# Fourier filter and two MLPs on one core: conversions leave the last column steps, and the way back follows the filter more closely

## The chip, the core and the metric

The kernel runs on one core of one Trainium2 chip. The time is that of one execution on the device, in microseconds; three runs of each kernel stand side by side, and the profile is that of one further execution. Engines are named as in the profile: PE is TensorE (PEld its weight loads), DVE is VectorE, ACT is ScalarE, POOL is GpSimd, SP the queue that issues most transfers.

## The reference, cut to what matters

```python
def _attn_ref(x, filt_r, filt_i):            # x: 4 x 3136 x 256
    X = np.fft.rfft(x, axis=1)
    F = (filt_r + 1j * filt_i)[None, :, :]
    return np.fft.irfft(X * F, n=x.shape[1], axis=1)

def _moe_ref(x, U, V, w_ch1, w_ch2):         # U: 3136 x 32, V: 32 x 3136, w: 256 x 1024 x 256
    h = x.transpose(0, 2, 1) @ U @ V
    u = x + h.transpose(0, 2, 1)
    return u + np.maximum(u @ w_ch1, 0.0) @ w_ch2

def _moe2_ref(x, g_ln, w_ch1, w_ch2):
    xn = (x - mean) / sqrt(var + 1e-6) * g_ln
    return x + np.maximum(xn @ w_ch1, 0.0) @ w_ch2
```

The three are applied one after the other. The weights and U, V come as 64-bit floats, seen by the kernel as pairs of 32-bit words.

## The kernel before

The transform of length 3136 is done as two stages of matmuls with tables, 28 groups of 112 positions. Batch 0 has a path of its own, the class `First`, in plain f32; batches 1 to 3 (`fft`) run later beside the MLPs. For batch 0 `rows` does the first stage and leaves its result in `big`, and `columns` does the second stage, the filter and the first half of the way back, two groups at a time: 14 pairs of groups.

A step j of `columns` has four parts. TensorE turns a pair back (line 502, `psz`), ScalarE copies it (`z0`). The pair turned in step j-1 goes through the table `e` (line 513, `ps2`), and `filt` copies its halves exchanged and negated on ScalarE (`xs` or `hh`) and multiplies `ps2` by the real filter on VectorE (line 225, into `ya` or `hl`; the tiles alternate). `total` multiplies the exchanged halves by the imaginary filter (line 492) and adds them (line 493), for the pair that was filtered one step earlier (`ADDL`). The way back multiplies a summed pair with the table in `d` (line 522, `ps3`, two halves of channels), copies the result into `big` on ScalarE, and adds up 64 columns on VectorE (line 528 the first time, then 530); `BACKL` says how late it is. Line 522 has the summed pair as its stationary operand, so a sum must be complete before it. In the first four steps `u_half` makes the spectrum of U (`pst`, line 462) for `uf`, from which ScalarE copies columns into `d`.

PSUM has eight banks: three in `ps_h`, four in `ps_o`, one in `ps_t`. Each engine runs its instructions in the order of the program; a matmul whose bank is still being read waits, and all behind it.

Weights are converted from 64-bit to 32-bit by a generator, `stagger`, which is called once for each *slot*. A job starts every four slots (`PACE`). In its first slot ScalarE reads the two words (lines 768 and 769), in the next four VectorE has one operation each (755, 757, 759, 761), with the last of them GpSimd multiplies (773), one slot later it adds (775); four slots on ScalarE copies the high part (`w1h`, `w2h`, `vh`), and in the next the low part is made on GpSimd (846, 885). So every fourth slot is a job change: a copy and two conversions on ScalarE, line 761, and three GpSimd operations that follow. `ROWSLOTS` and `COLSLOTS` say how many slots stand behind each step of `rows` and `columns`; the other slots stand in the long loop, one behind m1 and one at the end of each step.

The long loop runs 25 blocks of tokens through both MLPs, eight steps each: `m1` (six matmuls, `psh`, then `hh` on ScalarE and `hl` on VectorE), and `m2` of two steps before (`pso`). Between them stand the inverse transform of units of tokens (`psu`) and, early, the parts of batch 0 that are still to be turned (`psw`, `wt`, lines 572 and 574). Each w1b half is centred by two matmuls (line 855, `psw` from `wg`), which stand where the job's slot stands.

Of the kernel before, what the change touches and what calls it, by code (L numbers as in the profile page):

```python
# [10 lines left out]
F32 = mybir.dt.float32  # L11
# [9 lines left out]
P = 128  # L21
# [9 lines left out]

WARM, KEEP = 9, 2
ULAG, UTURN = 1, (0, 1, 2, 3)
ADDL, BACKL = 2, 4
AHEAD = 3
FETCHES = (0, 1, 3, 6)

SLOTS, UAHEAD = 8, 2
PACE = 4
ROWSLOTS = (0, 1, 1, 1, 1, 2, 2, 3, 3, 4, 4, 5)  # L40
COLSLOTS = (0, 0) + tuple(range(18))
VSTEP = 9
DIRECT = 4

# [94 lines left out]
def fft_mixer_kernel(ctx: ExitStack, tc: tile.TileContext, x, U, V, flt, w1, w2, gln, w1b, w2b,  # L139
# [7 lines left out]
    ps_h = ctx.enter_context(tc.tile_pool(name="ps_h", bufs=3, space=PSUM))  # L147
    ps_o = ctx.enter_context(tc.tile_pool(name="ps_o", bufs=4, space=PSUM))
    ps_t = ctx.enter_context(tc.tile_pool(name="ps_t", bufs=1, space=PSUM))
# [15 lines left out]
    def acopy(o, i, scale=1.0):  # L165
        nc.scalar.activation(out=o, in_=i, func=AF.Copy, scale=scale)  # L166
# [198 lines left out]
    class First:  # L365
# [76 lines left out]
        def u_half(self, h):  # L442

            if h:
                self.zs, uf = (mp.tile([P, 4 * D], F32, tag="x2t", name=nm, bufs=2)[:, :NM * R] for nm in ("zs", "uf"))
                self.uf = uf.rearrange("p (g r) -> p g r", r=R)
            n = 14 * R
            ps = ps_t.tile([P, 512], F32, tag="t", name="pst")
            for k in range(14):
                g = 14 * h + k  # L450
                nc.tensor.transpose(ps[:PP, k * R:(k + 1) * R], self.zu[:, g * PP:(g + 1) * PP], ident[:R, :R])
            zs = self.zs[:PP, h * n:(h + 1) * n]
            acopy(zs, ps[:PP, :n])
            yield
            ps = ps_t.tile([P, 512], F32, tag="t", name="pst")
            a = 0 if h else R
            if a:
                nc.tensor.matmul(ps[:, :a], self.e[:, 1], zs[:, :a], start=True, stop=True)
            nc.tensor.matmul(ps[:, a:n], self.e[:, 0], zs[:, a:], start=True, stop=True)
            for lo, hi, wc in ((14, 28, w_sb[:, 0:1]),) if h else ((0, 1, w_sb[:, 1:2]), (1, 14, w_sb[:, 0:1])):  # L460
                src = ps[:, (lo - 14 * h) * R:(hi - 14 * h) * R].rearrange("p (g r) -> p g r", r=R)
                nc.vector.tensor_scalar(out=self.uf[:, lo:hi], in0=src, scalar1=wc, scalar2=None, op0=ALU.mult)
# [14 lines left out]
        def columns(self):  # L477
# [17 lines left out]
            for j in range(n + BACKL):  # L495
                if j < n:
                    i = n - 1 - j
                    ps = ps_o.tile([P, 512], F32, tag="o", name="psz")
                    for g in range(2):
                        for dh in range(KT):  # L500
                            a = g * D + dh * P
                            nc.tensor.transpose(ps[:PP, a:a + P], self.big[:, dh, (2 * i + g) * PP:(2 * i + g + 1) * PP], ident)
                    zt[i] = wide(F32, "fin", "z0", D, 3)
                    acopy(flat(zt[i]), ps[:PP])
                if 0 < j <= n:
                    i = n - j
                    z = zt.pop(i)
                    ps = ps_h.tile([P, 512], F32, tag="h", name="ps2")
                    if i == 0:
                        for g in range(2):  # L510
                            nc.tensor.matmul(ps[:, g * D:(g + 1) * D], self.e[:, 1 - g], z[:, g], start=True, stop=True)
                    else:
                        nc.tensor.matmul(ps, self.e[:, 0], flat(z), start=True, stop=True)
                    sp.filt(i, ps, True)
                total(j)
                if j >= BACKL:
                    i = n + BACKL - 1 - j
                    ya = sp.y.pop(i)[0]
                    for dh in range(KT):
                        ps = (ps_h if dh else ps_o).tile([P, 512], F32, tag="h" if dh else "o", name="ps3")  # L520
                        for g in range(2):
                            nc.tensor.matmul(ps[:, g * w:(g + 1) * w], dealt(ya[:, g], dh), slot(2 * i + g),
                                             start=True, stop=True)
                        pv = ps[:, :2 * w].rearrange("p (g w) -> p g w", w=w)
                        acopy(self.big[:, dh, 2 * i * PP:2 * (i + 1) * PP].rearrange("p (g w) -> p g w", w=PP), pv[:, :, :PP])
                        acc = self.t[:, dh]
                        if j == BACKL:
                            nc.vector.tensor_copy(acc, pv[:, :, PP:])
                        else:
                            nc.vector.tensor_tensor(out=acc, in0=pv[:, :, PP:], in1=acc, op=ALU.add)  # L530
                if j in UTURN:
                    next(turns[UTURN.index(j) // 2], None)
                self.filters(j + AHEAD)
                if BACKL - UAHEAD <= j < n + BACKL - UAHEAD:
                    i = n + BACKL - UAHEAD - 1 - j
                    for g in () if i else range(2):
                        acopy(slot(g)[:, PP:w], self.uf[:, g])
                    if i:
                        g = 2 * i % SLOTS
                        acopy(d0[:, g:g + 2, PP:w], self.uf[:, 2 * i:2 * i + 2])  # L540
                yield j
# [352 lines left out]
    with tc.manual_schedule():  # L894
# [24 lines left out]
        for j in first.columns():  # L919
            for _ in range(COLSLOTS.count(j)):  # L920
                next(pr)
# [55 lines left out]
        for idx in range(len(steps) + 2):  # L977
            if idx < len(steps):
                ph, f = steps[idx]
                if ph[0] == "a" and f == 0:  # L980
                    units_to(need(ph[1]))
                m1(ph, f)
                load_to(emitted)
                next(pr, None)
                if idx > FFT0:
                    credit += RATE if 1 not in tstk else 0.4
                    if credit >= 1:
                        credit -= 1
                        next(rest, None)
            for act in todo.pop(0) if todo else ():  # L990
                act()
            if idx >= 2:
                m2(*steps[idx - 2])
                if steps[idx - 2][1] == FT - 1:
                    end(steps[idx - 2][0])
            if idx < len(steps):
                if f in (3, 6) and ph in ahead:
                    units_to(need(ahead[ph]), 1)
                if idx in PARTS:
                    next(later, None)  # L1000
                if idx == UPARTS:
                    first.u_parts()
                next(pr, None)
# [32 lines left out]
```

## Time and profile before

| | |
|---|---|
| median of three runs | 1381.7 us (1380.94 to 1382.22) |
| the profiled execution | 1380.91 us, span 1379.1 us |
| stage `rows` | until 34.3 us |
| stage `columns` | 34.3 to 91 us, 18 steps |
| first units and long loop | from 92.64 us |
| granted TensorE clock | 1.00 in nearly all of the span |

The span is what the trace covers; the rest of the time lies around it. Times in the text below are those of this execution, from the start of its span. In rows of the order of time a bracket at the end says how long the engine had stood idle before and whom it waited for.

### The profile page before, as it was taken

The numbers are of one execution on the slowest core, as the hardware profiler recorded it, in microseconds if no ns is written. First come the engines' busy times: TensorE is split into PE (matmuls) and PEld (weight loads), VectorE is DVE, ScalarE is ACT, GpSimd is POOL, SyncE is SP. The second block draws the span as 40 slices with busy tenths as digits, with TensorE's granted clock in tenths as the row PEclk, the third lists the DMA queues.
The fourth block names the chain that finished last, engine by engine and source line by source line (L and its number), as shares of the span: only waits on it lengthen the run. The fifth ranks groups of instructions, "written<-read, shape, count | busy, mean of one in ns | idle before, by whom it ended". The sixth has DMA issues, their size and how long they took to land.

```text
span 1379.1 us, 18643 instructions
## 1 busy us (share of the span) xinstructions
PE 1345.5 (98%) x6870; PEld 1122.9 (81%) x6870; DVE 822.9 (60%) x1642; ACT 555.9 (40%) x1048; POOL 151.1 (11%) x145
## 2 busy tenths in 40 slices
PE   8879999999999999999999999999999999999998
PEld 7568778877888887888888888888888888888887
DVE  4778975577555547666555557665455455544554
ACT  4865444466433334554333335554222222222221
POOL 2236611022000001111000001110000000000000
PEclk9999999999999999999999999999999999999999
DMA  9735356565535534543345355453112112200111
GB/s 268 264 97 139 88 132 190 156 178 165 141 93 146 135 81 129 153 134 100 80 127 142 91 137 147 126 153 81 25 52 65 35 37 79 66 18 29 46 47 39
DMA packets 141595, 152.20 MB, mean 110 GB/s; under 512 B 61472, under 2 KB 117696, under 8 KB 141408
## 3 DMA queue, kind: packets, MB, share of 16 engines
q1 hardware_dynamic: 134880, 139.72, 35.9%
q0 software_dynamic: 5760, 10.10, 3.3%
q8 instruction: 54, 0.88, 0.3%
q10 hardware_dynamic: 864, 1.20, 0.2%
q14 instruction: 37, 0.30, 0.1%
HBM read 103.44 MB, written 47.54 MB: 109 GB/s over the span
## 4 chain that ended last, share of the span: by engine, by line
PE 85%; DVE 7%; ACT 3%; DMA 3%; issue 2%; SPq 0%; POOL 0%; ACTq 0%; DVEq 0%; POOLq 0%
PE psh L632 36%; PE pso L659 12%; PE pso L660 6%; PE pso L651 6%; PE pso L652 6%; PE pso L653 6%; PE psu L603 3%; PE ps L198 2%; PE ps L199 2%; PE ps L200 2%; ACT xs L166 1%; DMA f<-flt 1%; DVE x2t L693 1%; PE psu L605 1%; DVE hl L636 1%
## 5 line engine op out<-in xcount | busy, mean ns | idle before, releaser
L636 DVE SCALAR_TENSOR_TENSOR hl<-psh,hh 128x512 fp32r<-128x512 f32 (+1 forms) x400 | 270.9, 678 | 408.8 <-ACT hh L635 408.3
L635 ACT ACTIVATE hh<-psh 128x512 fp32r<-128x512 f32 (+1 forms) x400 | 235.1, 588 | 624.6 <-PE psh L632 619.0
L659 PE MATMUL pso<-wb,hh 128*128 128x512 f32 x784 | 285.3, 397 | 0.8 <-DVE x L673 0.7
L632 PE MATMUL psh<-ah,wb 128*128 128x512 f32 (+1 forms) x800 | 277.0, 388 | 0.0
L660 PE MATMUL pso<-wb,hl 128*128 128x256 f32 x784 | 220.2, 281 | 0.6 <-DVE hl L636 0.6
L632 PEld LDWEIGHTS psh<-ah,wb 128*128 128x128 f32 x800 | 149.8, 188 | 33.1
L659 PEld LDWEIGHTS pso<-wb,hh 128*128 128x128 f32 x784 | 147.4, 188 | 35.0 <-DVE x L673 3.1
L651 PE MATMUL pso<-hh,w2h 128*128 128x512 f32 (+1 forms) x400 | 156.3, 391 | 1.0 <-DVE x2t L693 0.9
L652 PE MATMUL pso<-hl,w2h 128*128 128x512 f32 (+1 forms) x400 | 155.3, 388 | 1.3 <-DVE hl L636 1.1
L632 PE MATMUL psh<-ah,w1h 128*128 128x512 f32 (+1 forms) x400 | 155.7, 389 | 0.4 <-DVE hl L636 0.3
L632 PE MATMUL psh<-al,wb 128*128 128x512 f32 (+1 forms) x400 | 155.5, 389 | 0.0
L632 PE MATMUL psh<-al,w1h 128*128 128x512 f32 (+1 forms) x400 | 155.1, 388 | 0.0
L632 PE MATMUL psh<-ah,w1l 128*128 128x512 f32 (+1 forms) x400 | 154.8, 387 | 0.0
L653 PE MATMUL pso<-hh,w2l 128*128 128x512 f32 (+1 forms) x400 | 154.7, 387 | 0.0
L660 PEld LDWEIGHTS pso<-wb,hl 128*128 128x128 f32 x784 | 148.3, 189 | 6.9 <-DVE hl L636 1.2
L229 POOL TENSOR_TENSOR xs<-xs,ft 128x512 f32<-128x512 f32 x42 | 54.3, 1293 | 392.3 <-ACT xs L166 392.3
L651 PEld LDWEIGHTS pso<-hh,w2h 128*128 128x128 f32 x400 | 75.2, 188 | 19.1 <-issue 4.2
L652 PEld LDWEIGHTS pso<-hl,w2h 128*128 128x128 f32 x400 | 75.3, 188 | 17.1 <-DVE hl L636 3.4
L632 PEld LDWEIGHTS psh<-ah,w1h 128*128 128x128 f32 x400 | 75.3, 188 | 16.2 <-DVE hl L636 0.8
L632 PEld LDWEIGHTS psh<-ah,w1l 128*128 128x128 f32 x400 | 75.2, 188 | 15.8
L653 PEld LDWEIGHTS pso<-hh,w2l 128*128 128x128 f32 x400 | 75.2, 188 | 15.2
L632 PEld LDWEIGHTS psh<-al,w1h 128*128 128x128 f32 x400 | 75.3, 188 | 12.6 <-DVE al L169 0.2
(156 smaller groups left out, 1768.0 us busy)
## 6 DMA issues: line engine op xcount, KB each, us to landing
ft<-flt SPq DMA_DIRECT2D x42, 512.0 KB, 4.5
xd<-x SPq DMA_DIRECT2D x96, 128.0 KB, 2.9
x2t<-xd SPq DMA_DIRECT2D x24, 512.0 KB, 4.9
wt<-bd SPq DMA_DIRECT2D x24, 448.0 KB, 5.8
out<-x2t SPq DMA_DIRECT2D x84, 128.0 KB, 2.1
xt<-x SPq DMA_DIRECT2D x42, 224.0 KB, 3.7
zd<-ze SPq DMA_DIRECT2D x42, 224.0 KB, 2.7
zt<-zd SPq DMA_DIRECT2D x42, 224.0 KB, 3.3
```

The source lines that it names most:

```text
L198: nc.tensor.matmul(o, lh, rh, start=True, stop=False)
L199: nc.tensor.matmul(o, lh, rl, start=False, stop=False)
L229: nc.gpsimd.tensor_tensor(out=xs, in0=xs, in1=ft[:, :, 1], op=ALU.mult)
L603: nc.tensor.matmul(ps[:, m:UN:UW], t[:, m, dh * P:(dh + 1) * P], ic[:, m, :], start=m == 0, stop=False, skip_group_check=True)
L632: nc.tensor.matmul(ps[:, :n], w[:, kt, fs], a[:, kt, :n], start=j == 0, stop=j == 3 * KT - 1)
L635: nc.scalar.activation(out=hh[:, :n], in_=ps[:, :n], func=AF.Relu)
L636: nc.vector.scalar_tensor_tensor(out=hl[:, :n], in0=ps[:, :n], scalar=0.0, in1=f32(hh[:, :n]), op0=ALU.max, op1=ALU.subtract)
L651: nc.tensor.matmul(o, wh[:, f, ds], hh[:, :n], start=f == 0, stop=False)
L652: nc.tensor.matmul(o, wh[:, f, ds], hl[:, :n], start=False, stop=False)
L653: nc.tensor.matmul(o, wl[:, f, ds], hh[:, :n], start=False, stop=f == FT - 1)
L659: nc.tensor.matmul(o, hh[:, cs], w, start=f == 0, stop=False, skip_group_check=True)
L660: nc.tensor.matmul(o[:, D:], hl[:, cs], w[:, :D], start=False, stop=f == FT - 1, skip_group_check=True)
```

## The change

Four things change. `BACKL` becomes 3, so that the way back of a pair comes two steps behind its filter in place of three, and `columns` has 17 steps; `UAHEAD` follows, so that the copies from `uf` stay where they are. `COLSLOTS` has one slot behind step 0, two behind each of steps 1 to 4, one behind each of steps 5 to 12 and none behind 13 to 16: 17 in place of 20. The three that are left over run in the first four steps of the long loop, where `BUSY` makes three slots of two. And the second half of channels of the way back takes its bank from `ps_t` in odd steps, while the second `pst` of each half of U takes one of `ps_h`.

```diff
--- before.py
+++ after.py
@@ -31,14 +31,15 @@
 
 WARM, KEEP = 9, 2
 ULAG, UTURN = 1, (0, 1, 2, 3)
-ADDL, BACKL = 2, 4
+ADDL, BACKL = 2, 3
 AHEAD = 3
 FETCHES = (0, 1, 3, 6)
 
-SLOTS, UAHEAD = 8, 2
+SLOTS, UAHEAD = 8, 1
 PACE = 4
 ROWSLOTS = (0, 1, 1, 1, 1, 2, 2, 3, 3, 4, 4, 5)
-COLSLOTS = (0, 0) + tuple(range(18))
+COLSLOTS = (0, 1, 1, 2, 2, 3, 3, 4, 4) + tuple(range(5, 13))
+BUSY = 4
 VSTEP = 9
 DIRECT = 4
 
@@ -452,7 +453,7 @@
             zs = self.zs[:PP, h * n:(h + 1) * n]
             acopy(zs, ps[:PP, :n])
             yield
-            ps = ps_t.tile([P, 512], F32, tag="t", name="pst")
+            ps = ps_h.tile([P, 512], F32, tag="h", name="pst")
             a = 0 if h else R
             if a:
                 nc.tensor.matmul(ps[:, :a], self.e[:, 1], zs[:, :a], start=True, stop=True)
@@ -517,7 +518,8 @@
                     i = n + BACKL - 1 - j
                     ya = sp.y.pop(i)[0]
                     for dh in range(KT):
-                        ps = (ps_h if dh else ps_o).tile([P, 512], F32, tag="h" if dh else "o", name="ps3")
+                        pool, tag = ((ps_t, "t") if j % 2 else (ps_h, "h")) if dh else (ps_o, "o")
+                        ps = pool.tile([P, 512], F32, tag=tag, name="ps3")
                         for g in range(2):
                             nc.tensor.matmul(ps[:, g * w:(g + 1) * w], dealt(ya[:, g], dh), slot(2 * i + g),
                                              start=True, stop=True)
@@ -981,7 +983,8 @@
                     units_to(need(ph[1]))
                 m1(ph, f)
                 load_to(emitted)
-                next(pr, None)
+                for _ in range(2 if idx < BUSY else 1):
+                    next(pr, None)
                 if idx > FFT0:
                     credit += RATE if 1 not in tstk else 0.4
                     if credit >= 1:
```

What it moves, in the order in which the engines have their instructions (lines from 521 on stand two lower in the new text, those from 986 three, those before 521 one). On TensorE in the middle of the columns, numbers behind a name being buffers of the program, two steps before the change:

```order
L513 MATMUL ps2_729<-z0_695,e32_176 128x512
L522 MATMUL ps3_738<-d32_179,hl_635 128x144 x2
L522 MATMUL ps3_743<-d32_179,hl_635 128x144 x2
L502 MATMUL psz_760<-ident_79,big_183 112x128 x4
L513 MATMUL ps2_767<-z0_727,e32_176 128x512
L522 MATMUL ps3_776<-d32_179,ya_669 128x144 x2
L522 MATMUL ps3_781<-d32_179,ya_669 128x144 x2
```
and on VectorE the steps in which these tiles are filtered and summed:

```order
L225 TENSOR_TENSOR ya_669<-ps2_666,f0_549 128x512
L492 TENSOR_TENSOR hh_634<-hh_634,f0_515 128x512
L493 TENSOR_TENSOR hl_635<-hl_635,hh_634 128x512
L530 TENSOR_TENSOR d32_180<-ps3_675,d32_180 128x64
L530 TENSOR_TENSOR d32_180<-ps3_680,d32_180 128x64
L757 TENSOR_SCALAR ct_657<-cyh_619 128x512
L225 TENSOR_TENSOR hl_700<-ps2_697,f0_580 128x512
L492 TENSOR_TENSOR xs_668<-xs_668,f0_549 128x512
L493 TENSOR_TENSOR ya_669<-ya_669,xs_668 128x512
```
`hl_635` is summed in the step that filters `ps2_666`; line 522 reads it in the step of `ps2_729`, two later. With the change, TensorE:

```order
L514 MATMUL ps2_717<-z0_677,e32_176 128x512
L524 MATMUL ps3_726<-d32_179,hl_652 128x144 x2
L524 MATMUL ps3_731<-d32_179,hl_652 128x144 x2
L503 MATMUL psz_745<-ident_79,big_183 112x128 x4
L514 MATMUL ps2_752<-z0_715,e32_176 128x512
L524 MATMUL ps3_761<-d32_179,ya_682 128x144 x2
L524 MATMUL ps3_766<-d32_179,ya_682 128x144 x2
```
and VectorE:

```order
L226 TENSOR_TENSOR ya_682<-ps2_679,f0_561 128x512
L493 TENSOR_TENSOR hh_651<-hh_651,f0_525 128x512
L494 TENSOR_TENSOR hl_652<-hl_652,hh_651 128x512
L532 TENSOR_TENSOR d32_180<-ps3_688,d32_180 128x64
L532 TENSOR_TENSOR d32_180<-ps3_693,d32_180 128x64
L763 TENSOR_SCALAR cyh_571<-ct_609 128x512
L226 TENSOR_TENSOR hl_720<-ps2_717,f0_603 128x512
L493 TENSOR_TENSOR xs_681<-xs_681,f0_561 128x512
L494 TENSOR_TENSOR ya_682<-ya_682,xs_681 128x512
```
`hl_652` is summed in the step that filters `ps2_679`, and line 524 reads it in the step of `ps2_717`, the next one. The order within a step is as it was.

On VectorE at the end of the columns, from the last sum to the first copy of `psw`, before and with the change:

```order
L493 TENSOR_TENSOR ya_851<-ya_851,xs_850 128x512
L530 TENSOR_TENSOR d32_180<-ps3_879,d32_180 128x64
L530 TENSOR_TENSOR d32_180<-ps3_884,d32_180 128x64
L755 TENSOR_SCALAR cyh_871<-cyh_871 128x512
L530 TENSOR_TENSOR d32_180<-ps3_895,d32_180 128x64
L530 TENSOR_TENSOR d32_180<-ps3_900,d32_180 128x64
L757 TENSOR_SCALAR ct_893<-cyh_871 128x512
L530 TENSOR_TENSOR d32_180<-ps3_906,d32_180 128x64
L530 TENSOR_TENSOR d32_180<-ps3_911,d32_180 128x64
L759 SCALAR_TENSOR_TENSOR ct_893<-stg_758,ct_893 128x512
L574 COPY wt_917<-psw_926 112x4x128
```
```order
L494 TENSOR_TENSOR ya_870<-ya_870,xs_869 128x512
L532 TENSOR_TENSOR d32_180<-ps3_889,d32_180 128x64
L532 TENSOR_TENSOR d32_180<-ps3_894,d32_180 128x64
L532 TENSOR_TENSOR d32_180<-ps3_901,d32_180 128x64
L532 TENSOR_TENSOR d32_180<-ps3_906,d32_180 128x64
L576 COPY wt_911<-psw_920 112x4x128
```
The three conversion operations are gone from between the last additions, and so is one step's pair of additions behind the last sum.

At the start of the long loop on ScalarE, from `hh` of the first step, before and with the change:

```order
L635 ACTIVATE hh_1005<-psh_998 128x512
L166 ACTIVATE w1h_81<-ct_789 128x512
L768 ACTIVATE cyh_1012<-stg_875 128x512
L769 ACTIVATE cyl_1013<-stg_875 128x512
L166 ACTIVATE wt_1018<-psw_1021 112x4x128
L635 ACTIVATE hh_1044<-psh_1037 128x512
L166 ACTIVATE wt_1049<-psw_1052 112x4x128
L635 ACTIVATE hh_1072<-psh_1065 128x512
L166 ACTIVATE w2h_83<-ct_893 128x512
L768 ACTIVATE cyh_1079<-stg_1016 128x512
L769 ACTIVATE cyl_1080<-stg_1016 128x512
L166 ACTIVATE wt0_1093<-psw_1094 112x512
```
```order
L637 ACTIVATE hh_999<-psh_992 128x512
L167 ACTIVATE wt_1008<-psw_1011 112x4x128
L637 ACTIVATE hh_1031<-psh_1024 128x512
L167 ACTIVATE w1h_81<-ct_741 128x512
L770 ACTIVATE cyh_1038<-stg_837 128x512
L771 ACTIVATE cyl_1039<-stg_837 128x512
L167 ACTIVATE wt_1048<-psw_1051 112x4x128
L637 ACTIVATE hh_1071<-psh_1064 128x512
L167 ACTIVATE w2h_83<-ct_1005 128x512
L770 ACTIVATE cyh_1079<-stg_1042 128x512
L771 ACTIVATE cyl_1080<-stg_1042 128x512
L167 ACTIVATE wt0_1093<-psw_1094 112x512
```
`w2h` keeps its place behind `hh` of step 2, while the two conversions ahead of it (`w1h` and what follows) stand one step later. On VectorE, from `hl` of the first step, before and with the change:

```order
L636 SCALAR_TENSOR_TENSOR hl_1006<-psh_998,hh_1005 128x512
L761 TENSOR_SCALAR cyh_871<-ct_893 128x512
L574 COPY wt_1018<-psw_1027 112x4x128
L755 TENSOR_SCALAR cyh_1012<-cyh_1012 128x512
L636 SCALAR_TENSOR_TENSOR hl_1045<-psh_1037,hh_1044 128x512
```
```order
L638 SCALAR_TENSOR_TENSOR hl_1000<-psh_992,hh_999 128x512
L757 TENSOR_SCALAR cyh_833<-cyh_833 128x512
L759 TENSOR_SCALAR ct_1005<-cyh_833 128x512
L576 COPY wt_1008<-psw_1017 112x4x128
L761 SCALAR_TENSOR_TENSOR ct_1005<-stg_708,ct_1005 128x512
L638 SCALAR_TENSOR_TENSOR hl_1032<-psh_1024,hh_1031 128x512
L763 TENSOR_SCALAR cyh_833<-ct_1005 128x512
```
Line 761 of the job whose high part is this `w2h` (`ct_893`, now `ct_1005`) stood behind `hl` of step 0 and stands behind that of step 1, as line 763.

## Rows read from the trace of the kernel before

**Rows 1.** The page, part 1: busy us, share of span, instructions.

```profile
PE 1345.5 (98%) x6870; PEld 1122.9 (81%) x6870; DVE 822.9 (60%) x1642; ACT 555.9 (40%) x1048; POOL 151.1 (11%) x145
```

**Rows 2.** VectorE in order of time: start, us, engine, line, operation, tiles.

```profile
49.97 0.68 DVE L225 TENSOR_TENSOR ya<-ps,f 128x512 f32<-128x512 f32 x1
...
63.29 0.68 DVE L225 TENSOR_TENSOR ya<-ps,f 128x512 f32<-128x512 f32 x1
...
68.60 0.69 DVE L225 TENSOR_TENSOR ya<-ps,f 128x512 f32<-128x512 f32 x1
...
76.64 0.68 DVE L225 TENSOR_TENSOR ya<-ps,f 128x512 f32<-128x512 f32 x1
...
81.95 0.69 DVE L225 TENSOR_TENSOR ya<-ps,f 128x512 f32<-128x512 f32 x1
```

**Rows 3.** VectorE in order of time, one product held up.

```profile
72.94 1.50 DVE L492 TENSOR_TENSOR xs<-xs,f 128x512 f32<-128x512 f32 x1
```

**Rows 4.** The loop's links in order of time: TensorE, ScalarE, VectorE; brackets: idle before, releaser.

```profile
53.32 1.15 PE L522 MATMUL ps<-d,hl 128*128 128x144 f32 x8
...
54.30 0.60 PE L502 MATMUL psz<-ident,big 128*112 128x128 f32 x4
...
54.91 1.10 PE L513 MATMUL ps<-z,e 112*128 112x512 f32 x2
...
63.19 1.10 PE L513 MATMUL ps<-z,e 112*128 112x512 f32 x2 [1.41 <-DVE d L530]
...
58.55 1.19 ACT L166 ACTIVATE hh<-ps 64x512 f32<-64x512 f32 x2
...
64.32 1.19 ACT L166 ACTIVATE hh<-ps 64x512 f32<-64x512 f32 x2 [0.84 <-PE ps L513]
...
59.83 0.69 DVE L225 TENSOR_TENSOR hl<-ps,f 128x512 f32<-128x512 f32 x1 [1.95 <-POOL cyl L773]
...
63.89 0.68 DVE L492 TENSOR_TENSOR hh<-hh,f 128x512 f32<-128x512 f32 x1
...
64.61 0.69 DVE L493 TENSOR_TENSOR hl<-hl,hh 128x512 f32<-128x512 f32 x1
...
65.22 0.35 DVE L530 TENSOR_TENSOR d<-ps,d 128x64 f32<-128x64 f32 x2
```

**Rows 5.** The end of the columns in order of time.

```profile
86.93 1.23 PE L522 MATMUL ps<-d,ya 128*128 128x144 f32 x8 [1.60 <-issue]
...
87.02 1.23 DVE L755 TENSOR_SCALAR cyh<-cyh 128x512 f32<-128x512 f32 x1
...
88.12 1.19 PE L572 MATMUL psw<-ident,big 128*112 128x128 f32 x8
...
90.44 0.68 DVE L574 COPY wt<-psw 112x512 f32<-112x512 f32 x1
```

**Rows 6.** Waits of TensorE, 30 to 98 us: us in total, times, longest.

```profile
PE ps L513 <- DVE d L530: 3.7, 2, 2.2
...
PE pst L451 <- DVE uf L462: 1.4, 1, 1.4
```

**Rows 7.** The start of the long loop in order of time.

```profile
101.28 0.42 DVE L761 TENSOR_SCALAR cyh<-ct 128x512 int32<-128x512 int32 x1
...
103.27 0.69 DVE L636 SCALAR_TENSOR_TENSOR hl<-psh,hh 128x512 fp32r<-128x512 f32 x1 [0.64 <-ACT hh L635]
...
106.48 0.67 ACT L166 ACTIVATE w2h<-ct 128x512 fp32r<-128x512 f32 x1 [1.33 <-POOL ct L775]
...
108.19 0.57 ACT L166 ACTIVATE wt<-psw 112x512 f32<-112x512 f32 x1
...
110.48 1.04 PE L603 MATMUL psu<-ic,wt 112*128 112x112 f32 x8
```

**Rows 8.** TensorE in order of time: a centring matmul.

```profile
158.88 1.13 PE L855 MATMUL psw<-wg,ones 128*128 128x512 f32 x2 [1.42 <-DVE wg L836]
```

**Rows 9.** One stretch: busy us by engine (instructions), then granted clock, DMA share, GB/s.

```profile
92.00:96.00 4.00, 4.00 (x23) 3.96 (x23) 1.57 (x3) 2.10 (x5) 0.00 (x0) 0.57 0.36 125
```
## The prediction

> **What bounds the kernel now.** The page first: over the whole span TensorE is busy 98% [rows 1], so almost all of the program is TensorE's own pace, and a delay that is put in ahead of that stretch is carried to the end. The change edits the stage in front of it, the columns of batch 0 (34 to 91 us), and the first four steps of the long loop behind. VectorE's order of time shows the pace of the columns by line 225, which stands once in each step [rows 2]: the filter of step 4 starts at 49.97 and that of step 14 at 81.95, ten steps in 31.98 us. They come in two kinds. The pair from 63.29 to 68.60 takes 5.31, and there are three such pairs; the pair from 68.60 to 76.64 takes 8.04, and there are two (the other is what is left of 49.97 to 63.29, 8.01). In the long pairs a conversion job changes over: ScalarE has two conversions and a copy on top, and VectorE's products and sums of two SBUF operands stand still while GpSimd works, 1.50 instead of 0.68 [rows 3]. In the short pairs VectorE has no gap: 0.60 (63.29 to 63.89) for line 225, 0.72 for 492, 0.6 for 493, 0.35 for the pair of 530 [rows 4], and a conversion operation. So VectorE sets the short steps, and neither TensorE nor the way back is waited for in them.
>
> **The way back moves one step nearer to the sum.** Now TensorE's line 522 in step j reads a product that line 493 summed in step j-2; afterwards it reads the one of step j-1. Both engines work in program order, so a loop closes that goes round once in two steps. Its links, each from a row [rows 4]: line 522's eight records until the transposes 0.98 (53.32 to 54.30); transposes until line 513 0.61; line 513 until ScalarE's negated copies 1.13 (63.19 to 64.32); those copies until line 225 1.28 (58.55 to 59.83); 225 to 492 0.60 and 492 to 493 0.72; line 493 itself 0.69 until the next line 522. That is 6.01, and with 0.1 for the step from VectorE back to TensorE 6.1 for two steps, against 5.31 now. The order before had three steps for the same 6.1, or 2.0 a step, which is why it shows no such wait. VectorE's own work is below that, so it will idle some 0.3 to 0.4 us in a step.
>
> The two slots in the first steps shift the job changes: they fell behind steps 6, 10 and 14 and now fall behind 4, 8 and 12. So between step 4 and step 14 there are three long pairs and two short ones. Short: 2 x 6.1 = 12.2. A long pair is at least what it is now, 8.0, when job change and loop overlap; at most 6.1 and the whole of what a job change adds now (8.04 - 5.31 = 2.73), 8.8. Some of the job change lies in the loop (the sum that stands still, the copies that wait for ScalarE) and some beside it, so I take the middle, 8.4; three make 25.2. Ten steps: 37.4, that is **+5.4** (bounds +4.2 and +6.6).
>
> **The end of the columns.** Now from line 225 of step 14 (81.95) to the first copy of line 574 (90.44) it is 8.49 us, because lines 755, 757 and 759 stand between the last line 530s and the copy, 755 alone with 1.23 while GpSimd works [rows 5]. Afterwards none stands there, and one step of way back is gone: lines 225, 492, 493 and 530 of step 14, 492 and 493 of step 15: 0.60 + 0.72 + 0.60 + 0.35 + 0.72 + 0.69 = 3.7; then the last line 522 to the end of the transposes, 86.93 to 89.31 = 2.4 [rows 5]. Together 6.1, **-2.4**; with one more sum held by GpSimd (0.8, as in [rows 3]) -1.6.
>
> **The beginning.** The second bank for `pst` takes away TensorE's wait of 1.4 for line 462 [rows 6]; lines 755 and 757 move behind the first filter. ScalarE's job change behind step 2 stays where it is, and line 225 of step 3 waited for ScalarE. I take **0**; bounds -1.4 (the whole wait) and +0.8 (one more operation held by GpSimd).
>
> **Queues that the slots pass.** A slot carries more than VectorE's operation: loads of the next weights on SP's queue, three GpSimd operations and two conversions a job, and the writes of `vd` on ScalarE's. The number of job changes in the columns stays five, so ScalarE and GpSimd do the same there. On SP a load of weights waits for line 759 of an older job with the filter loads behind it; line 759 stands earlier by as many steps as the load: 0.
>
> **Eight banks.** TensorE's line 513 waited 3.7 us in two places for line 530, which gives a `ps_h` bank free [rows 6]. With `ps_t` taking every second result these go. Both fell in long pairs, where VectorE and ScalarE were behind as well; the loop above takes their place, so I count nothing beyond the lower bound of a long pair.
>
> **The long loop.** Three conversion slots that stood at the end of the columns now run at its start, under TensorE. But three slots to a step bring the stages of a job nearer to each other: line 761 stood behind `hl` of step 0 (101.28) and now stands behind that of step 1 (103.27 and 0.60), 2.6 later, while ScalarE's `w2h` keeps its place behind `hh` of step 2. Between line 761 and `w2h` lie three GpSimd operations, and ScalarE already waited 1.33 for them (106.48). It will wait longer, and behind it stands the copy of `psw` (108.19, 0.57) whose bank TensorE's second `psu` group takes at 110.48 [rows 7]: slack 1.7. So 2.6 - 1.7 = **+0.9** on TensorE; bounds 0 (GpSimd is earlier done with older work) and 2.6. The centring matmuls of line 855 move from behind m1 to ahead of it. The second pair waits 1.42 now [rows 8], with VectorE behind; the first will wait for line 673 in exchange: 0, bounds 1.4 either way.
>
> **The clock.** The granted clock is 0.57 on average from 92 to 96 [rows 9], which costs 4 x 0.43 = 1.7 us; it followed on the idle end of the columns, when TensorE had waited for line 549. Such an idle end remains, a little shorter: 0, bounds -1.7 and +1.7.
>
> **Sum.** 5.4 - 2.4 + 0 + 0.9 + 0 = +3.9 us. The profiled execution took 1380.9 (span 1379.1 and 1.8 around it), the median of the runs is 0.8 above it; on the median, 1381.7 + 3.9 = 1385.6.
>
> **Rivals.** *Faster: the banks were the limit.* If the loop does not bind (its links shorten when TensorE has nothing else, or line 522's first half hides in front of the sum), short pairs keep 5.31 and the long ones lose the 3.7 us of bank waits: 2 x 5.3 + 3 x 6.2 = 29.2, -2.8; with the end -2.4 and the long loop +0.9 it is 1377.4. It decides where a short pair comes out under 5.6. For it: the waits for line 530 are there, and TensorE is far from full. Against: six of the seven links are queue order on one engine, and none shrinks when idle. Here the Trainium skill speaks against my forecast: "Perfetto Trace Analysis" (section Matmul Optimizations) asks that all eight banks be used so that more can overlap. By that rule this edit is a gain; the rows show that only the long pairs wait for a bank.
>
> *No change.* The low end of the ten steps (+4.2), the end (-2.4) and the whole wait at the beginning (-1.4) leave 0.4, and the long loop hides its part: 1382.1. For it: each of these is a plain reading of one row.
>
> *Much slower: ScalarE's queue.* If `w2h` costs TensorE the whole 2.6 and the next job, packed as tightly, as much again, and the centring 1.4: 5.4 - 2.4 + 5.2 + 1.4 = +9.6, 1391.3. For it: ScalarE waits there already. Against: from the fifth step on it is two slots again.
>
> *The clock falls inside the columns.* TensorE's part of the loop (0.98 + 0.61 + 0.93) doubles in five pairs: +12.6 beside the forecast's 3.9, 1398.2. Against: busy shares like those now kept full clock there until 92. The Trainium skill, "TensorE: Matmul & The Clock Gate" (section What's actually happening), makes the throttled state the resting one, which activity releases; the low stretch behind the idle end agrees.
>
> **Chances.** Forecast 0.58, faster 0.10, no change 0.17, ScalarE's queue 0.12, clock 0.03. Within 0.2% (2.8 us), about what a measurement of this kernel can tell from no change, lie the third and 0.08 of the forecast: 0.25; slower 0.65, faster 0.10. The forecast's own range is 1382.5 to 1389; with most of the dear rival and the case of no change 1379.5 to 1391.5, which leaves out the gain and the clock.
>
> **What would show it.** Line 225 to line 225 over two short steps near 6.1, and line 522 waiting for line 493 in most steps, is the loop; 5.3 with no such wait refutes it, and with it the sign. No TensorE wait for line 530. Line 574 some 6 us behind the last line 225. In the loop, ScalarE's wait ahead of the first `w2h` above 3 us and TensorE waiting once in the `psu` group of step 3. Wrong it would be, above all, if the long pairs shrink, or if the long loop takes back what the columns lose.

## The result: 11.4 us slower, three times the forecast

The changed kernel takes 1392.76 us (median of four runs, 1391.05 to 1393.42), the kernel before beside it 1381.32 (four runs, 1380.69 to 1382.22): ratio 1.0083, 95% interval 1.007 to 1.0096. The sign was forecast, the size was not: +11.4 in place of +3.9, and 1.3 us beyond the end of the range. The profiled execution took 1391.05 with a span of 1389.3, 10.2 more than that of before.

VectorE in order of time, every second filter from step 4 on (line 226, as in [rows 2]), then the first copy of `psw` (line 576, was 574 in [rows 5]):

```profile
52.40 0.69 DVE L226 TENSOR_TENSOR ya<-ps,f 128x512 f32<-128x512 f32 x1 [0.97 <-ACT xs L167]
...
61.13 0.68 DVE L226 TENSOR_TENSOR ya<-ps,f 128x512 f32<-128x512 f32 x1
...
69.03 0.68 DVE L226 TENSOR_TENSOR ya<-ps,f 128x512 f32<-128x512 f32 x1
...
77.08 0.68 DVE L226 TENSOR_TENSOR ya<-ps,f 128x512 f32<-128x512 f32 x1
...
83.29 0.68 DVE L226 TENSOR_TENSOR ya<-ps,f 128x512 f32<-128x512 f32 x1
...
90.96 0.67 DVE L226 TENSOR_TENSOR ya<-ps,f 128x512 f32<-128x512 f32 x1
...
99.48 0.69 DVE L576 COPY wt<-psw 112x512 f32<-112x512 f32 x1 [0.60 <-PE psw L574]
```

Ten steps take 90.96 - 52.40 = 38.56 us (31.98 before). The short pair from 77.08 to 83.29 takes 6.21, as the loop said. The other short pair, 61.13 to 69.03, takes 7.90, and the end, 90.96 to 99.48, has lost nothing: 8.52 (8.49 before). TensorE's waits from 30 to 98 us (us in total, times, longest), to be held against [rows 6]:

```profile
PE ps L524 <- DVE d L532: 9.5, 5, 3.3
PE ps L524 <- DVE ya L494: 3.2, 1, 3.2
PE ps L524 <- issue: 1.7, 1, 1.7
PE ps L524 <- DVE hl L494: 1.4, 3, 0.9
```

No `ps2` waits for line 532 any more. What is waited for now is the sum: line 524 stood idle behind VectorE nine times, for up to 3.3 us in one piece (line 532, where it is named, is the instruction right behind the sum, and the two end within 0.4 us). What these pieces do is seen on TensorE in order of time (the bracket is its idle time ahead of the row):

```profile
44.50 2.26 PE L524 MATMUL ps<-d,hl 128*128 128x144 f32 x8 [1.73 <-issue]
...
60.76 1.81 PE L524 MATMUL ps<-d,ya 128*128 128x144 f32 x8 [3.34 <-DVE d L532]
...
76.71 1.23 PE L524 MATMUL ps<-d,ya 128*128 128x144 f32 x8 [3.00 <-DVE d L532]
...
90.92 1.27 PE L524 MATMUL ps<-d,ya 128*128 128x144 f32 x8 [3.17 <-DVE ya L494]
...
93.11 2.26 PE L524 MATMUL ps<-d,hl 128*128 128x144 f32 x8 [0.92 <-DVE hl L494]
```

The same eight matmuls take 1.23 us or 2.26. Around the long ones the granted clock is at its lower level (stretches: the columns are as in [rows 9]):

```profile
44.00:51.00 7.00, 6.50 (x19) 4.67 (x20) 4.84 (x11) 4.26 (x9) 2.96 (x3) 0.51 0.35 131
60.70:64.00 3.30, 3.24 (x13) 2.80 (x14) 3.00 (x9) 1.40 (x4) 0.00 (x0) 0.58 0.99 390
92.00:98.00 6.00, 4.52 (x18) 4.00 (x17) 3.15 (x9) 1.86 (x8) 0.00 (x0) 0.50 0.00 0
```

0.50 is 1.2 GHz of 2.4. These three stretches lie behind idle places of 1.73, 3.34 and 3.17 us; behind the 3.00 at 76.71 the clock did not fall. The kernel before stood at 1.00 in all of the columns and fell only at 92 us [rows 9]:

```profile
30.00:60.00 30.00, 25.01 (x162) 17.76 (x159) 18.23 (x37) 23.21 (x50) 8.31 (x8) 1.00 0.79 269
60.00:70.00 10.00, 8.19 (x47) 5.93 (x46) 9.86 (x21) 8.95 (x24) 2.19 (x3) 1.00 0.87 302
70.00:80.00 10.00, 6.60 (x36) 4.71 (x35) 8.81 (x18) 7.79 (x19) 4.20 (x3) 1.00 0.48 117
80.00:90.00 10.00, 5.96 (x41) 5.06 (x39) 9.89 (x22) 6.31 (x17) 4.66 (x3) 1.00 0.27 93
```
The first units, which ran in the low stretch in that execution of the kernel before, ran at full clock in this one: from the first copy of `psw` to step 0 of the long loop 6.42 us (99.48 to 105.90), 7.95 before. Whether the change did this is not shown: one and the same kernel below (the banks alone) has 8.03 in one profile and 6.44 in another.

The long loop, first matmul of step 0 and of step 19, in the kernel after:

```profile
105.90 0.40 PE L634 MATMUL psh<-ah,w1h 128*128 128x512 f32 x1
...
173.82 0.39 PE L634 MATMUL psh<-ah,w1h 128*128 128x512 f32 x1
```
and in the kernel before:

```profile
98.39 0.40 PE L632 MATMUL psh<-ah,w1h 128*128 128x512 f32 x1
...
163.97 0.39 PE L632 MATMUL psh<-ah,w1h 128*128 128x512 f32 x1
```
67.92 against 65.58: +2.3. ScalarE's first `w2h` in order of time, the row that answers to [rows 7]:

```profile
116.43 0.67 ACT L167 ACTIVATE w2h<-ct 128x512 fp32r<-128x512 f32 x1 [3.39 <-POOL ct L777]
```

### The profile page after: what moved, and what is told of

Read it like the earlier page. It is cut to its first block, busy times and chain, and to the rows that moved or that the text cites. A ratio compares the mean times of both kernels' runs of the same rounds, so it can differ in the third digit from the quotient of the medians.

```text
span 1389.3 us, 18642 instructions
## 1 busy us (share of the span) xinstructions
PE 1350.6 (97%) x6870; PEld 1125.0 (81%) x6870; DVE 822.7 (59%) x1642; ACT 556.7 (40%) x1048; POOL 148.3 (11%) x145
## 4 chain that ended last, share of the span: by engine, by line
PE 83%; DVE 7%; ACT 3%; DMA 3%; issue 2%; SPq 0%; POOL 0%; ACTq 0%; DVEq 0%; POOLq 0%
PE psh L634 35%; PE pso L661 12%; PE pso L662 6%; PE pso L653 6%; PE pso L654 5%; PE pso L655 5%; PE psu L605 3%; PE ps L199 2%; PE ps L201 2%; PE ps L200 2%; DVE hl L638 1%; ACT xs L167 1%; DMA x<-x 1%; PE ps L524 1%; DVE x2t L695 1%
```

## The experiments

Each kernel ran beside the kernel before on one chip; times are medians, "over before" is the difference of the two medians, the interval that of the ratio. The kernels below were measured on four chips, on which the median of the kernel before lay between 1381.37 and 1382.76; the result above has runs of its own.

| kernel | us | over before | ratio, 95% |
|---|---|---|---|
| changed, way back three steps behind | 1382.66 | +1.0 | 0.9989 to 1.001 |
| way back alone | 1384.78 | +3.1 | 1.0014 to 1.0033 |
| banks alone | 1379.72 | -2.0 | 0.9974 to 0.9993 |
| slots alone | 1384.77 | +3.1 | 1.0009 to 1.003 |
| way back and slots | 1393.16 | +10.4 | 1.0055 to 1.0088 |
| way back and banks | 1384.98 | +2.2 | 1.0006 to 1.0025 |
| changed, TensorE kept busy | 1387.35 | +4.6 | 1.0021 to 1.0053 |
| the same in the last three steps only | 1389.15 | +7.8 | 1.0036 to 1.0064 |
| banks, no slots in the last steps | 1382.26 | -0.5 | 0.999 to 1.0015 |
| changed, two slots in every loop step | 1406.27 | +24.9 | 1.0163 to 1.0191 |
| that, way back three steps behind | 1395.63 | +14.3 | 1.009 to 1.0118 |
| banks, TensorE kept busy at the end | 1380.67 | -0.7 | 0.9984 to 1.0004 |
| changed, sum ahead of the filter | 1383.03 | +0.9 | 1.0001 to 1.002 |
| way back, banks, sum ahead | 1378.67 | -3.5 | 0.9968 to 0.9986 |
| banks, sum ahead | 1378.33 | -3.8 | 0.9964 to 0.9983 |
| banks alone, again | 1380.56 | -1.6 | 0.9977 to 0.9998 |

Stage by stage, each from one profiled execution (us; beginning: filter of step 1 to that of step 4; ten steps: on to that of step 14; end: on to the first copy of `psw`; first units: on to step 0 of the long loop; loop: step 0 to step 19):

| kernel | beginning | ten steps | end | first units | loop | sum over before |
|---|---|---|---|---|---|---|
| before | 10.28 | 31.98 | 8.49 | 7.95 | 65.58 | |
| changed | 11.88 | 38.56 | 8.52 | 6.42 | 67.92 | +9.0 |
| way back three behind | 10.56 | 32.72 | 7.53 | 6.43 | 67.51 | +0.5 |
| way back alone | 10.57 | 38.05 | 8.99 | 8.39 | 65.58 | +7.3 |
| slots alone | 11.08 | 35.68 | 6.09 | 6.37 | 67.60 | +2.5 |
| banks alone | 9.78 | 31.55 | 8.50 | 8.03 | 65.55 | -0.9 |
| banks alone, again | 9.77 | 31.55 | 8.52 | 6.44 | 65.58 | -2.4 |
| way back and slots | 11.17 | 39.44 | 9.60 | 6.35 | 67.53 | +9.8 |
| way back and banks | 10.18 | 38.19 | 8.90 | 6.42 | 65.55 | +5.0 |
| TensorE kept busy | 10.84 | 36.62 | 6.37 | 6.42 | 67.77 | +3.7 |
| kept busy in the last three steps | 10.83 | 40.56 | 6.37 | 6.42 | 67.58 | +7.5 |
| two slots in every loop step | 10.83 | 40.37 | 9.01 | 8.63 | 85.59 | +30.2 |
| sum ahead of the filter | 10.78 | 32.59 | 6.67 | 6.43 | 67.60 | -0.2 |
| banks, sum ahead | 9.80 | 30.45 | 7.34 | 6.42 | 65.58 | -4.7 |

What lies outside differs too: the filter of step 1 starts between 38.0 and 41.9 us in the profiles although the program up to there is nearly the same; the stages above don't carry that. They do carry the clock. Up to the filter of step 14 the changed kernel has the same instructions as the one kept busy in the last three steps and the one with two slots in every loop step, and the ten steps took 38.56, 40.56 and 40.37 in the three profiles: where the clock falls differs from execution to execution. At full clock the stages repeat closely (31.55 twice for the banks alone).

**One part undone or done alone.** Way back three steps behind in the changed kernel:

```diff
-ADDL, BACKL = 2, 3
+ADDL, BACKL = 2, 4
-SLOTS, UAHEAD = 8, 1
+SLOTS, UAHEAD = 8, 2
```


> The changed kernel with the way back put back to three steps behind the filter; slots and banks stay as changed. Theory 'loop': the sum that line 524 waits for is long done, so that wait (9.5 us from 30 to 98 us) is gone, a short pair of filters takes 5.3 again in place of 6.2, the ten steps lose 5 to 6.6 of their 38.6 us, and the granted clock stays up between 60 and 90 us; about 1384 to 1386. Theory 'slots' (the two slots of the first steps and the busier start of the long loop do it): it stays at 1390 or above. Theory 'banks' (results of the way back hold a bank that something else needs): it stays at 1390 or above as well.

+1.0: theory "loop", and even better than it said. Ten steps 32.72 in place of 38.56. One part of it did not come: the clock is 0.55 from 81 to 88 us in this profile too, at the end of the columns.

The way back alone has the two numbers of that diff the other way round and `COLSLOTS = (0, 0) + tuple(range(17)) + (16,)`:

> The kernel before with the way back two steps behind the filter and nothing else (20 slots still stand in the columns, the last step has two). Theory 'loop': three short pairs grow from 5.3 to 6.1 and two long ones by 0 to 0.8, the ten steps take 2.4 to 4 us longer, one step of way back less at the end saves 1 to 2; with low clock at idle places up to 3 more: 1384 to 1389. Theories 'slots' and 'banks': no loss, 1380 to 1382.

+3.1, in the range. Its profile is the slowest of its ten runs (1387.77), and there the ten steps grew by 6.1, which takes in most of the 3 that the range had set aside for low clock: the short pairs from step 8 to 10 and from 12 to 14 took 7.5 and 8.5, with the clock down. The banks alone, the `ps3` and `pst` lines of the change:

> The kernel before with the changed banks alone. Theory 'loop': the waits of line 513 for line 530 (3.7 us) and of pst (1.4) go, some of it comes out as time: 1378 to 1381.5. Theory 'banks': 1385 or above.

-2.0, and -1.6 when repeated:

> The kernel before with the changed banks alone, once more: -1 to -3 (it gave -2.0, interval -3.6 to -1.0).

The slots alone, `COLSLOTS`, `BUSY` and the loop over `range(2 if idx < BUSY else 1)`:

> The kernel before with the changed slots alone (17 in the columns, the three others in the first four steps of the long loop). Theory 'loop': the end of the columns gains up to 2.4 since no conversion stands between the last additions, the long loop loses about 2.4 as in the changed kernel: 1380 to 1384. Theory 'slots': 1389 or above, with the columns themselves longer by some 6 us.

+3.1. The filter of step 14 and the first copy of `psw` on VectorE:

```profile
86.29 0.68 DVE L226 TENSOR_TENSOR ya<-ps,f 128x512 f32<-128x512 f32 x1
...
92.38 0.69 DVE L575 COPY wt<-psw 112x512 f32<-112x512 f32 x1 [0.53 <-PE psw L573]
```
That is 0.8 above the range. The end takes 6.09 us, the forecast's 6.1, though the forecast reached it with one step of way back less, which this kernel does not have; the ten steps take 3.7 more, with the third long pair and a stretch of low clock (0.83 from 70 to 80 us), and the long loop 2.0.

The parts add up to 3.1 - 2.0 + 3.1 = +4.2, close to the forecast; the whole is +11.4. So by the medians two of them must meet:

> The changed kernel with the banks put back as before: way back and slots together. Alone the way back gave +3.1 and the slots +3.1. Theory 'sum': the parts add up, about 1388. Theory 'together': long pairs and loop meet three times in the ten steps and TensorE's idle times there let the granted clock fall, so the two cost more together than apart: 1391 to 1395, with low clock inside the columns.

> The kernel before with the way back nearer and the changed banks, slots as before. Alone +3.1 and -2.0. Theory 'sum': 1382 to 1384. Theory 'together' puts the dear part on way back and slots, so the same here. Rival 'banks meet loop' (with a free bank TensorE runs ahead and then waits in one long piece for the sum): 1387 or above.

+10.4 and +2.2 (1.0 above the range): by the medians it is way back and slots that cost 4.2 more together than apart (some 1 to 7, with the three intervals taken together), with the banks free of blame. The table of stages puts this excess at the end. In the ten steps the two cost 7.5 together, 6.1 and 3.7 apart. At the end the slots alone gain 2.4 and the way back alone loses 0.5; together they lose 1.1, and with the banks the gain is gone as well. Low clock inside the columns comes with each of them alone already: way back alone, way back and banks (a profile at the median of its runs), slots alone:

```profile
80.00:90.00 10.00, 7.70 (x33) 6.01 (x31) 6.89 (x16) 6.33 (x16) 0.00 (x0) 0.74 0.03 7
```
```profile
65.00:75.00 10.00, 9.10 (x42) 6.45 (x42) 6.44 (x16) 7.77 (x18) 1.00 (x2) 0.81 0.51 129
```
```profile
40.00:50.00 10.00, 9.13 (x42) 6.37 (x43) 6.98 (x15) 7.26 (x15) 2.96 (x3) 0.66 0.61 238
```
With the slots alone it fell behind waits of 1.41 us for line 463 and 2.22 for a bank (line 531), so not only behind waits for the sum.

**TensorE kept busy.** The changed kernel with matmuls whose result is overwritten unread:

```diff
+HOLD = {3: 6, 6: 10, 10: 10, 14: 10, 15: 4, 16: 2}
...
                         ps = pool.tile([P, 512], F32, tag=tag, name="ps3")
+                        for _ in range(0 if dh else HOLD.get(j, 0)):
+                            nc.tensor.matmul(ps[:, :P], ones, ones, start=True, stop=True)
```


> The changed kernel with matmuls that nothing reads (ones by ones, 128x128, in the bank that the way back then overwrites) in front of line 524 in the steps where TensorE waits for the sum: 6 in step 3, 10 in steps 6, 10 and 14, 4 in step 15, 2 in step 16. They fit into waits of 1.7 to 3.3 us. Theory 'clock' (a part of the loss is half clock after these waits, about 4 us by rows: line 524 2.26 in place of 1.23 in the last three steps and similar rows at 44 to 51 and 61 to 64): low stretches in the columns go, 1387 to 1390. Theory 'loop alone' (half clock falls where TensorE is waited for little): 1391 to 1394.

+4.6, so more work on TensorE made the kernel some 6 us faster than the change (ratio 1.0037 in place of 1.0083, the intervals apart). VectorE's filters in order of time, steps 4, 6, 8, 10, 12 and 14, then the copy (its lines stand one to three lower):

```profile
51.57 0.68 DVE L227 TENSOR_TENSOR ya<-ps,f 128x512 f32<-128x512 f32 x1
...
60.05 0.68 DVE L227 TENSOR_TENSOR ya<-ps,f 128x512 f32<-128x512 f32 x1
...
66.25 0.68 DVE L227 TENSOR_TENSOR ya<-ps,f 128x512 f32<-128x512 f32 x1
...
74.30 0.68 DVE L227 TENSOR_TENSOR ya<-ps,f 128x512 f32<-128x512 f32 x1
...
80.51 0.68 DVE L227 TENSOR_TENSOR ya<-ps,f 128x512 f32<-128x512 f32 x1
...
88.19 0.67 DVE L227 TENSOR_TENSOR ya<-ps,f 128x512 f32<-128x512 f32 x1
...
94.56 0.69 DVE L579 COPY wt<-psw 112x512 f32<-112x512 f32 x1 [0.53 <-PE psw L577]
```
Both short pairs now take 6.2, the long ones 8.48, 8.05 and 7.68, the end 6.37. TensorE and the clock there, in order of time and as two stretches:

```profile
88.14 1.23 PE L527 MATMUL ps<-d,ya 128*128 128x144 f32 x8 [0.96 <-DVE ya L495]
89.21 1.05 PE L525 MATMUL ps<-ones 128*128 128x128 f32 x8
90.33 1.23 PE L527 MATMUL ps<-d,hl 128*128 128x144 f32 x8
```
```profile
44.00:51.00 7.00, 4.74 (x29) 3.41 (x29) 4.87 (x11) 5.53 (x12) 2.98 (x3) 1.00 0.43 162
88.00:94.00 6.00, 5.67 (x41) 5.18 (x42) 4.49 (x13) 2.52 (x9) 0.00 (x0) 1.00 0.00 0
```
The way back takes 1.23 everywhere, the clock is 1.00. Only the last three entries of `HOLD` left:

> The changed kernel with the unread matmuls only in the last three steps (10 in step 14, 4 in 15, 2 in 16), none in steps 3, 6 and 10. With all of them the loss fell to +4.6 over the kernel before. Theory 'the end is the dear one' (three line 524 groups of 2.26 in place of 1.23 and what follows them): full clock from 90 us on, line 226 of step 14 to the first copy of psw near 6.4, +6.5 to +8.5. Theory 'the middle is the dear one' (44 to 51 and 61 to 64 us): +9 to +11.5.

+7.8: the end is regained (6.37 in its profile), the middle is not. By the medians roughly half of the loss to the clock lies in each. TensorE in this profile at the two places that lie ahead of its unread matmuls, with the instructions of the changed kernel (line 524 is 527 here):

```profile
45.14 1.23 PE L527 MATMUL ps<-d,hl 128*128 128x144 f32 x8 [1.73 <-issue]
...
76.78 2.26 PE L527 MATMUL ps<-d,ya 128*128 128x144 f32 x8 [2.96 <-DVE d L535]
```
Behind the 1.73 the clock stayed up here and fell in the changed kernel's profile; behind the 2.96 it fell here and stayed up there. The profile with two slots in every loop step has the same two as here.

**The loop itself.** One line of the changed kernel moved, so that VectorE sums the pair before ahead of the filter:

```diff
+                total(j)
                 if 0 < j <= n:
                     i = n - j
...
                     sp.filt(i, ps, True)
-                total(j)
```


> The changed kernel with one line moved: in each step VectorE makes the sum of the pair before (lines 493, 494) ahead of the filter (line 226) in place of behind it. Line 524 then reads a sum that no longer stands behind the filter of the step before, and the loop goes round in three steps. Theory 'loop': short pairs 5.3 to 5.5 in place of 6.2, ten steps 34 to 36, less idle TensorE and higher clock, +4 to +8 over before. Rival 'nearer as such' (the stalls of GpSimd reach TensorE whatever the order on VectorE): +9.5 to +12.

+0.9, better than either theory said. TensorE's two largest waits from 30 to 98 us, and VectorE's filters of steps 4, 10, 12 and 14:

```profile
PE ps L524 <- DVE hl L494: 4.6, 5, 2.1
PE ps L524 <- ACT d L167: 4.1, 5, 0.9
```
```profile
51.58 0.68 DVE L226 TENSOR_TENSOR ya<-ps,f 128x512 f32<-128x512 f32 x1
...
72.03 0.68 DVE L226 TENSOR_TENSOR ya<-ps,f 128x512 f32<-128x512 f32 x1
...
77.34 0.68 DVE L226 TENSOR_TENSOR ya<-ps,f 128x512 f32<-128x512 f32 x1
...
84.17 0.68 DVE L226 TENSOR_TENSOR ya<-ps,f 128x512 f32<-128x512 f32 x1
```
The short pair is 5.31 again, to the hundredth what it was in [rows 2], the longest wait for a sum 2.1 in place of 3.3, and the ten steps take 32.59. The same order with other parts:

> Nearer way back and changed banks with the slots of before (alone +2.2) and the sum ahead of the filter. Theory 'loop': pace of the columns as with the banks alone, one step of way back less at the end, -1 to -4. Rival 'nearer as such': +1.5 to +3.

> Changed banks alone, with the sum ahead of the filter, way back three steps behind. No loop binds there, so the order gives nothing: -1 to -3, as the banks alone. If it comes out faster by 2 us more, the order is worth something by itself.

-3.5 and -3.8. The nearer way back is free once the filter is out of the loop. The control came out otherwise than expected, though: the order is worth 2 us without any loop as well (-3.8 against -2.0 and -1.6 for the banks alone), so of the 10.5 us that it gave the changed kernel some 2 are its own. The last of these is the fastest version found.

**The long loop.** The changed kernel with `BUSY = 0`:

> The changed kernel with two slots in every step of the long loop as before (none of the first four has three), so every later job stands three slots later. In the changed kernel and its variants with three slots, step 19 of the long loop begins 67.5 to 67.9 us behind step 0, in those without 65.6. Theory 'packed slots': 65.6 again and 2.3 us less, +8 to +9.5 over before. Rival 'what is converted late costs as much': a later weight is waited for, step 19 at 67 or more, +10.5 or more.

+24.9, far on the rival's side, and the same without the nearer way back:

> The changed kernel with way back three steps behind the filter and with two slots in every step of the long loop: first steps of the columns with two slots and the changed banks are all that is left. With three slots it stood at +1.0. Theory 'packed slots': 2.3 less, -1 to -1.5. Rival as in the run beside it: +0.5 to +1.5.

+14.3, far beyond both of its theories. TensorE's largest wait in the first, from 110 to 200 us:

```profile
PE pso L655 <- POOL w2l L848: 6.1, 3, 2.2
```
The low part of a `w2` quarter is not there when m2 wants it, three times. From step 0 to step 19 this loop takes 85.59 in place of 67.92, and these 6.1 are only a part of the 17.7. The granted clock fell there too, to 0.92 on average (1.00 in the changed kernel); 0.08 of 85.59 is some 6.8 us more by estimate, and the rest was not followed up. (Later steps give a part back: the span is 27.0 longer than before, the stages 30.2.) So the three slots that left the columns had to be made up at once; packing them is the cheaper way, and about 2 us its price. Banks alone with `COLSLOTS = (0, 0) + tuple(range(15))` and the packed start:

> The kernel before with the changed banks and no conversion slots in the last three column steps; the three slots stand in the first four steps of the long loop; way back three steps behind, first steps with their slots as before. Banks alone gave 1379.7. If the end of the columns gains its 2.4 us (6.1 from the last line 226 to the first copy of psw) and the busier start of the long loop costs about 0.4 to 1: 1377.5 to 1379. If the long loop takes the gain back: 1379.5 to 1382.

-0.5: it lost what the banks had gained. The end took 7.39 us at full clock, 1.1 better and not 2.4, less than the packed start costs: 2 us in the kernels above, 3.7 in this profile (step 0 to step 19 69.25).

The last one fills TensorE's idle places in a kernel without the loop, `HOLD = {15: 6, 16: 6, 17: 6}` on the banks alone and eight such matmuls ahead of `pst` in `mixed`:

> The kernel before with the changed banks and unread matmuls where TensorE is idle at the end of the columns (6 in each of the last three steps in front of the way back, 8 in front of pst of mixed). Banks alone gave -2.0. Theory 'clock': psu runs at full clock (4.4 us to step 0 of the long loop in place of 5.8), -3 to -3.5. Rival 'filled idle time delays what follows': -2 to 0.

-0.7, with an interval from -2.2 to +0.6: theory "clock" with its -3 is out. Its profile shows the first units at full clock (4.40 us from the first `psu` to step 0, 5.83 with the banks alone), but so does the second profile of the banks alone, without any filling (4.42). In the changed kernel filling paid, at the end of its columns too; here no gain was shown.

## Why the prediction was right in sign and wrong in size

**The loop of the way back (+5.4): right.** Its two short pairs were to take 6.1; they take 6.20 and 6.21 at full clock. The long pairs were to take 8.4 each; they took 8.07 on average. Without low clock that is +4.6, with it +6.6. Taking the filter out of the loop brought the pair back to 5.31.

**The end (-2.4): right by itself, and not seen.** 6.37 with TensorE kept busy, against 6.1 forecast (the 6.09 of the slots alone belongs to another order); 8.52 in the changed kernel, where the last two pieces of way back took 2.26 and 2.29 in place of 1.23, at 1.2 GHz.

**The clock (0, bounds 1.7): this step failed.** It said that "such an idle end remains, a little shorter", and looked at one place, the old idle end. The forecast had worked out that TensorE would wait for the sum, but it spread this wait evenly ("some 0.3 to 0.4 us in a step" for VectorE) and asked nowhere how long the single waits would be. They gather in the long pairs, where a sum held up by GpSimd (line 494 took 1.64 at 74.92, as in [rows 3]) now reaches TensorE one step later, with no slack: 3.0 to 3.3 us in one piece. There the clock fell, in the columns and ahead of the end. The low clock cost 1.0 at the beginning, 1.9 in the ten steps and 2.2 at the end (changed against TensorE kept busy, table of stages), 5.1 together in that execution; by the medians some 6. In the profile with two slots in every loop step, whose columns have the same instructions, it was 0, 3.8 and 2.6, and 2.2 more in the first units. The rival "the clock falls inside the columns" had the mechanism and a chance of 0.03. It was put aside because "busy shares like those now kept full clock there until 92": the shares were those of a kernel in which line 513's longest wait for VectorE was 2.2 us [rows 6]. Its price, 12.6, was too high, since not all five pairs ran slow. The rival "ScalarE's queue" named 1391.3, only 1.5 below the measured time, but by another way: it put +6.6 on the long loop and its centring, which took +2.3.

The Trainium skill had the sentence to weigh: "Perfetto Trace Analysis" (section Matmul Optimizations) says that the engine scales its power with utilization and that matmuls should therefore execute back to back in batches. The rows agree: the same eight matmuls 1.23 or 2.26, and unread ones in the gaps made the kernel faster.

**The long loop (+0.9, bounds 0 and 2.6): right in mechanism, too small.** The price fell due as worked out: `w2h` waits 3.39 (over 3 was forecast), and step 4 of the loop begins 0.9 later than before (14.09 against 13.19 behind step 0). But the packed jobs charge again: step 5 begins 1.3 later than before, step 7 2.3. (Step 11 begins 3.6 later, because the first centring, line 857, now stands ahead of its m1; by step 12 1.0 of that is given back.) +2.3 at step 19, and 1.9 to 2.3 in every kernel of the table of stages with the packed start.

**The beginning (0): +0.6** at full clock, inside its bounds; +1.6 as it ran. **Eight banks (nothing): -1.6 to -2.0** alone. The waits of `ps2` for line 530 did go, and unlike what I assumed, something came out where no loop takes their place; where one does, way back and slots with the banks (+11.4) and without (+10.4, on another chip) can't be told apart. The Trainium skill's sentence that all eight banks be used ("Perfetto Trace Analysis", section Matmul Optimizations), weighed in the prediction, agrees with the banks alone.

With the clock held, the stages add up to +3.7, near the forecast's +3.9, though two misses cancel in it (first units at full clock -1.5, long loop 1.3 above its term). The parts taken one by one add up to +4.2. What a sum of parts can't show is what they do together. Each of way back and slots brings the clock down inside the columns by itself; what they add in company is only seen in part. The slots put the third long pair ahead of the end, the way back lets it reach TensorE, and the 3.17 us of idle time in front of the last way back is followed by the low clock that takes the end's gain. Which of the idle places tips the clock stays open: the same instructions with the same idle time were followed by 1.23 in one execution and 2.26 in another. Whether the length of a single wait decides, or all of the idle time around it, no run here separates.

## What to carry to other kernels

When a change turns slack into a wait on TensorE, list the single waits as well as their mean: a long one may be paid a second time in the clock of what follows, and a gain that stands right behind it is lost with it. Before moving a consumer nearer, look at what stands between producer and consumer on their engine; here one line that put the sum ahead of the filter gave back what the whole change had lost. And conversions taken out of a stage that waits have to go somewhere by a due time: price that place as well.

## What was not expected of the hardware

Runs of the kernel before spread by 8 us (1378.61 to 1386.52), and a part of that goes with the granted clock of the span: over 99 runs the median is 1380.8 us where the mean clock is 0.996 or more (39 runs) and 1383.3 where it is 0.991 or less (24 runs). That is 2.5 us, 0.2%, as much as a single part of this change.

Matmuls whose result is thrown away made the changed kernel some 6 us faster.
